# Low half of a third quarter of w_out on VectorE, and all operations in a new order

## The chip, the cores and the metric

The kernel runs on one core of a Trainium2 chip. The metric is the time on the device in microseconds (us), the median of several executions; lower is better. A core has five engines that work side by side and meet at semaphores: TensorE (PE, matrix products, with its weight loads shown apart as PEld), VectorE (DVE), ScalarE (ACT), GpSimd (POOL) and SyncE (SP), which here issues every DMA. Each engine runs its own instructions in the order in which they stand in the program.

## The reference

The inputs are q, k, v (8 batches, 8 heads, 576 positions, 64 wide), w_in (512 x 1024), w_out (1024 x 512) and g_ln (1024). k and v are averaged over groups of 8 positions, so that each head has 72 keys; then comes attention, and its output, 4608 rows of 512, goes through a SoLU layer:

```python
scores = scale * q @ k_pooled.T
attn = softmax(scores)
x = attn @ v_pooled                    # 4608 x 512 after the heads are put side by side
h = x @ w_in                           # 4608 x 1024
solu = h * softmax(h)
ln = (solu - mean(solu)) / sqrt(var(solu) + 1e-6) * g_ln
out = ln @ w_out                       # 4608 x 512
```

## The kernel before

The 4608 rows are worked on in 36 tiles of 128 rows. A group of nine tiles holds two batches: four tiles of the first, one mixed tile with the last 64 rows of both, four of the second. Every product that needs more than 16-bit accuracy is made of float16 halves: an operand X is kept as X_hi and X_lo = X - X_hi, and a product is the sum of hi·hi, lo·hi and hi·lo.

**A tile** goes through: `q_hi`, `q_lo`, `q_T` (split q, transpose it by DMA), `scores`, `s_max`, `s_sub`, `s_exp`, `e_sum`, `e_rec`, `e_mul` (softmax), `e_hi`, `e_lo`, `e_T` (split and transpose), `av` (attention times v), `x_hi`, `x_lo`, `mm1` in three parts of 16 matmuls (tile h in a buffer `hp`, of which there are two), `h_max`, `h_nb`, `h_exp`, `z_scale`, `z_mul`, `z_cen`, `z_hi`, `z_lo`, `z_T`, `z_var`, `n_u`, `n_f`, `mm2` in three parts, `o_evac`, `o_store`. Tiles overlap: scores of a tile run some tiles ahead of its `mm1`, and `mm2` some behind.

**The weights** arrive as 64-bit floats, seen as pairs of 32-bit words, a quarter (c = 0 to 3) at a time: `w_load` (1024 KB), then `w_exp`, `w_shift`, `w_tail`, `w_sgn`, `w_mul` make 32-bit floats of them; `w_bnd`, `w_rmax`, `w_par`, `w_all` and `wi_scale` or `wo_scale` find a power of two that bounds all four quarters. Then `w_hi` writes the high half. For the low half there are two ways:

- `w_res` and `w_lo`: TensorE forms w·scale - w_hi in PSUM, by a product with a diagonal matrix (`w_dg`, made by ScalarE) and one with minus the identity (`minus`), and ScalarE copies it to float16;
- `w_lod`: VectorE forms it directly, one `scalar_tensor_tensor` for each half of 512 columns, all three tensors in SBUF.

Which quarter takes which way is in the set `LO_DVE`: before, quarters 2 and 3 of w_out go by VectorE, all other six by TensorE. Pooled k and v of batch 0 are summed by TensorE (`pool_pe`, with copies `pool_ev` by ScalarE), those of later batches by GpSimd (`pool_kv`).

**The order** is written out by hand as a table: `ORDER[name]` gives each call of a step its place in one list of some 2080 steps. The steps are sorted by it and issued one after the other, so that the table alone sets what stands behind what on each engine. A step is one to some hundred instructions. SP's queue is in the same order, and a DMA that waits holds up all DMAs behind it. The tag "raw" has seven buffers, shared by four quarters of w_out, two of w_in and the raw k and v of each batch; a load into one waits until its last reader is done.

Of the kernel before, what the change touches and what calls it, by code (L numbers as in the profile page):

```python
# [30 lines left out]
        "a_unit.k": (39, 57, 211, 213, 451, 455, 657, 663, 882, 890, 1129, 1155, 1390, 1437, 1615,
        1616),
        "a_unit.v": (131, 134, 254, 261, 500, 503, 804, 805, 1027, 1029, 1180, 1181, 1481, 1482,
        1804, 1805),
        "av": (215, 257, 276, 333, 383, 463, 506, 573, 561, 661, 775, 702, 842, 893, 952, 977,
        1012, 1111, 1189, 1206, 1287, 1327, 1398, 1433, 1512, 1546, 1628, 1684, 1651, 1756, 1785,
        1852, 1920, 1939, 1997, 1972),
        "e_T": (221, 239, 275, 332, 402, 425, 572, 497, 628, 712, 641, 761, 825, 873, 933, 957,
        1078, 1145, 1146, 1248, 1263, 1356, 1406, 1476, 1495, 1557, 1647, 1634, 1718, 1748, 1851,
        1887, 1908, 1996, 1942),  # L40
# [18 lines left out]
        "e_sum": (91, 139, 185, 253, 311, 367, 412, 498, 437, 538, 655, 612, 704, 772, 817, 888,  # L59
        926, 1023, 1106, 1049, 1200, 1238, 1274, 1345, 1425, 1379, 1502, 1581, 1564, 1655, 1704,  # L60
        1784, 1824, 1864, 1954, 1917),
        "g_T": (93,),
        "g_all": (122,),
        "g_max": (96,),
        "g_par": (121,),
        "g_put": (94,),
        "h_bat": (245, 283, 679, 904, 1060, 1182, 1535, 1839),
        "h_exp": (265, 325, 362, 441, 457, 545, 614, 623, 697, 751, 857, 828, 936, 954, 1005,
        1037, 1151, 1185, 1258, 1300, 1384, 1402, 1486, 1510, 1612, 1618, 1679, 1796, 1720, 1832,
        1875, 1925, 1989, 1979, 2040, 2022),  # L70
        "h_max": (256, 305, 347, 411, 454, 525, 585, 619, 660, 719, 838, 777, 917, 941, 979, 1028,
        1130, 1159, 1231, 1268, 1309, 1389, 1456, 1489, 1551, 1610, 1673, 1733, 1703, 1798, 1846,
        1913, 1947, 1965, 2038, 2011),
# [161 lines left out]
def kernel(  # L235
# [48 lines left out]
    wo = const.tile([P, 2, CO, DM], F16, name="wo")  # L284
# [1073 lines left out]
    LO_DVE = {("wo", 2), ("wo", 3)}  # L1358
# [191 lines left out]
```

## Time and profile before

| | before |
|---|---|
| median of 3 executions | 487.48 us (487.16 to 487.89) |
| span of the profiled execution, first to last instruction | 483.6 us |
| what lies around the span, taken as median less span | 3.9 us |
| TensorE busy | 456.5 us |
| VectorE busy | 372.2 us |
| ScalarE busy | 335.2 us |
| GpSimd busy | 304.5 us |

The profile has no time of its own for the profiled execution beside its span. The three executions lie within 0.15% of each other, so the span and 3.9 us around it are read as one of them. A row of a timeline gives start, duration, engine, line, operation, written and read tiles, and in brackets the idle time before it with what ended it.

### The profile page before, as it was taken

Reading aid. Unit: us, or ns where it says so; the run is one execution under the profiler, and the core shown is the slowest. Engines: PE = TensorE matmul, PEld = TensorE weight load, DVE = VectorE, ACT = ScalarE, POOL = GpSimd, SP = SyncE. Lnnn points to the kernel's source line nnn. Section 1 sums busy time; section 2 is a strip of 40 time slices with the busy share of each in tenths; the row PEclk is TensorE's granted clock in tenths of the full one; section 3 lists DMA queues with packets and bytes.
Section 4 is the critical chain, followed back from the end, with each engine's and each line's share of the span. In section 5 each row is a group of like instructions: output and inputs, shape, how many; then the busy total and the mean of one; then the engine's idle time right before and its main releaser. Section 6 shows DMA issues by size and latency. Waiting matters only on the chain.

```text
span 483.6 us, 14740 instructions
## 1 busy us (share of the span) xinstructions
PE 456.5 (94%) x5976; PEld 287.7 (59%) x5976; DVE 372.2 (77%) x787; ACT 335.2 (69%) x557; POOL 304.5 (63%) x525
## 2 busy tenths in 40 slices
PE   1779899999999999999999999999999999999996
PEld 1655455655655556555556667666776666755553
DVE  5988999999889789878798867678878887462320
ACT  5598887677966688796677657587585697456361
POOL 3459737696697985858953597717758625643532
PEclk9989999999999999999999999999999999999999
DMA  8999389998999899999994999689899576861742
GB/s 309 395 354 225 86 114 219 196 193 138 213 237 213 209 173 207 204 229 229 161 215 111 215 245 172 126 136 243 167 229 190 115 137 117 138 142 24 153 108 69
DMA packets 197749, 88.92 MB, mean 184 GB/s; under 512 B 174121, under 2 KB 182321, under 8 KB 197169
## 3 DMA queue, kind: packets, MB, share of 16 engines
q1 hardware_dynamic: 197680, 87.98, 85.9%
q8 instruction: 47, 0.77, 0.6%
q14 instruction: 22, 0.17, 0.1%
HBM read 36.70 MB, written 9.44 MB: 95 GB/s over the span
## 4 chain that ended last, share of the span: by engine, by line
PE 78%; DVE 16%; DMA 2%; issue 2%; ACT 1%; SPq 0%; POOL 0%; ACTq 0%; DVEq 0%
PE op L274 35%; PE hp L274 31%; PE xp L999 4%; PE sc L274 3%; DMA kr<-in_k_dram 2%; DVE q L866 2%; DVE m L1041 1%; PE krps L410 1%; DVE sc L934 1%; DVE mx L920 1%; DVE sc L923 1%; DVE z L1073 1%; DVE e L949 1%; PE vrps L410 1%; PE res_wi L810 1%
## 5 line engine op out<-in xcount | busy, mean ns | idle before, releaser
L274 PE MATMUL hp<-wi,xT 128*64 128x512 f16 x1728 | 197.2, 379 | 2.8 <-DVE z L1073 1.4
L274 PE MATMUL op<-wo,zT 128*64 128x512 f16 x1728 | 197.2, 379 | 0.1
L274 PEld LDWEIGHTS <-xT 128*64 128x64 f16 x1728 | 106.6, 110 | 75.2 <-ACT xT L1008 2.0
L274 PEld LDWEIGHTS <-zT 128*64 128x64 f16 x1728 | 106.5, 110 | 70.6 <-DMA zT<-z 0.5
L1093 POOL TENSOR_TENSOR z<-z,z 128x512 f16<-128x512 f32 x71 | 82.0, 1167 | 67.9 <-ACT z L1087 66.4
L978 POOL TENSOR_TENSOR e<-e,e 128x512 f16<-128x512 f32 x36 | 42.2, 1173 | 39.7 <-ACT e L972 39.6
L1041 DVE TENSOR_REDUCE m<-hp 128x1 f32<-128x1024 f32 x36 | 43.8, 1217 | 23.1 <-PE hp L274 22.9
L1082 ACT ACTIVATE z<-z,sz 128x1024 f32<-128x1024 f32 x36 | 41.2, 1143 | 17.4 <-DVE z L1073 17.4
L1073 DVE SCALAR_TENSOR_TENSOR z<-hp,rs,z 128x1024 f32<-128x1024 f32 x36 | 46.1, 1280 | 9.1 <-ACT z L1052 7.9
L1052 ACT ACTIVATE z<-hp,nb,Hb 128x1024 f32<-128x1024 f32 x32 | 38.3, 1196 | 11.7 <-DVE nb L1044 9.1
L1151 ACT ACTIVATE osb<-op,f 128x512 f32<-128x512 f32 x36 | 24.5, 679 | 31.3 <-PE op L274 8.1
L1087 ACT ACTIVATE z<-z 128x1024 f16<-128x1024 f32 x36 | 37.7, 1050 | 0.9 <-DMA zT<-z 0.4
L1106 ACT ACTIVATE junk<-z 128x1024 f16<-128x1024 f32 x36 | 37.7, 1048 | 0.3
L400 POOL TENSOR_TENSOR vr<-vr 128x512 f32<-128x512 f32 (+3 forms) x42 | 36.9, 888 | 0.6
L400 POOL TENSOR_TENSOR kr<-kr 128x512 f32<-128x512 f32 (+3 forms) x42 | 36.7, 882 | 1.0 <-DMA kr<-in_k_dram 0.2
L920 DVE TENSOR_REDUCE mx<-sc 128x8 f32<-128x576 f32 x36 | 27.0, 750 | 12.9 <-PE sc L274 12.6
L934 DVE TENSOR_REDUCE sc<-sc 128x8 f32<-128x576 f32 x36 | 27.3, 759 | 12.2 <-ACT sc L930 12.1
L999 PEld LDWEIGHTS <-vb 128*64 128x64 f16 x960 | 28.9, 111 | 6.7 <-DVE vb L574 1.0
L1012 DVE SCALAR_TENSOR_TENSOR xT<-xp,xT 128x512 f16<-128x512 f32 x36 | 24.5, 681 | 8.9 <-ACT xT L1008 8.8
L999 PE MATMUL xp<-eT,vb 128*64 128x128 f16 (+1 forms) x960 | 31.0, 215 | 0.3 <-ACT e L975 0.3
L274 PEld LDWEIGHTS <-qT 128*64 128x64 f16 x1152 | 24.7, 114 | 9.9 <-ACT dg_wi L803 3.4
L1008 ACT ACTIVATE xT<-xp 128x512 f16<-128x512 f32 x36 | 21.2, 589 | 12.2 <-PE xp L999 12.2
(237 smaller groups left out, 621.3 us busy)
## 6 DMA issues: line engine op xcount, KB each, us to landing
kr<-in_k_dram SPq DMA_DIRECT2D x16, 512.0 KB
qr<-in_q_dram SPq DMA_DIRECT2D x16, 512.0 KB
vr<-in_v_dram SPq DMA_DIRECT2D x16, 512.0 KB
out_dram<-osb SPq DMA_DIRECT2D x32, 256.0 KB
wor<-in_moe_w_out_dram SPq DMA_DIRECT2D x4, 1024.0 KB
wo<-in_moe_w_in_dram SPq DMA_DIRECT2D x2, 1024.0 KB
wir<-in_moe_w_in_dram SPq DMA_DIRECT2D x2, 1024.0 KB
zT<-z SPq DMA_TRANSPOSE x72
```

The costliest lines, as they stand in the source:

```text
L274: nc.tensor.matmul(out[lo : lo + 64] if m > 64 else out, lhsT=lhsT[:, lo : lo + 64], **kw)
L400: nc.gpsimd.tensor_tensor(out=dst, in0=src[:, :, :n], in1=src[:, :, n : 2 * n], op=ALU.add)
L934: nc.vector.tensor_reduce(out=tl[i]["r0"], in_=s_view(i), axis=AX.X, op=ALU.add)
L978: nc.gpsimd.tensor_tensor(out=e_main(i, 1), in0=e_src(i)[0], in1=e_main(i, 0), op=ALU.subtract)
L999: nc.tensor.matmul(xp[64 * e : 64 * e + 64, c, lo:hi], lhsT=vb[b % 2][:, n, c, e], rhs=eT[:, 2 * c + e if n < 2 else H + e, lo:hi], start= ...
L1041: nc.vector.tensor_reduce(out=small(i, "m"), in_=tl[i]["hp"], axis=AX.XY, op=ALU.max)
L1052: nc.scalar.activation(z, t["hp"], AF.Exp, bias=t["nb"], scale=hsc(i, 0), accum_out=small(i, "se"))
L1073: nc.vector.scalar_tensor_tensor(out=t["z"], in0=t["hp"], scalar=t["rs"], in1=t["z"], op0=ALU.mult, op1=ALU.mult, accum_out=small(i, "sz"),)
L1082: nc.scalar.activation(t["zf"], t["zf"], AF.Identity, bias=t["sz"], scale=-float(DFF))
L1087: nc.scalar.activation(t["z16"][:, 0], t["zf"], AF.Copy)
L1093: eng.tensor_tensor(out=t["z16"][:, 1, fs], in0=t["zf"][:, fs], in1=t["z16"][:, 0, fs], op=ALU.subtract)
L1106: nc.scalar.activation(junk, t["zf"], AF.Square, scale=DFF**-0.5, accum_out=small(i, "V"))
```

## The change

`LO_DVE` also holds quarter 1 of w_out. For that quarter the program no longer has `w_dg` (two ScalarE instructions), `w_res` (TensorE) and `w_lo` (one ScalarE instruction), and has two `w_lod` on VectorE. The table `ORDER` is another one: from the first step to about the middle of the list steps stand in other places; the last 141 of TensorE's 338 steps, the last 246 of VectorE's 716 and the last 160 of ScalarE's 439 follow each other as before. Line numbers of the new program are 5 higher from the end of the table on. Of the table two lines are shown:

```diff
-        "w_lod.wo": (344, 324, 321, 316),
-        "w_res.wo": (210, 173),
+    "w_lod.wo": (217, 215, 258, 319, 303, 318),
+    "w_res.wo": (197,),
...
     POOL_SIGN = {(nm, c) for nm in ("wi", "wo") for c in range(4)}
-    LO_DVE = {("wo", 2), ("wo", 3)}
+    LO_DVE = {("wo", 1), ("wo", 2), ("wo", 3)}
     Q_ABS = {("b", b) for b in range(0)}
```

SP at the start of the program, before (`wo` is the buffer that two quarters of w_in are loaded into, `wir` are the other two, `wor` quarters of w_out, `kr`, `vr`, `qr` raw k, v and q of batch 0):

```order
L623 DMA wo<-in_moe_w_in_dram 128x2048 x2
L360 DMA kr_158<-in_k_dram 64x512
L623 DMA wir_169<-in_moe_w_in_dram 128x2048
L356 DMA kr_158<-in_k_dram 128x2x512 x2
L376 DMA qr_182<-in_q_dram 128x4x256 x2
L623 DMA wir_222<-in_moe_w_in_dram 128x2048
L623 DMA wor_288<-in_moe_w_out_dram 128x2x1024
```

The same place now:

```order
L628 DMA wo<-in_moe_w_in_dram 128x2048 x2
L365 DMA kr_146<-in_k_dram 64x512
L628 DMA wir_160<-in_moe_w_in_dram 128x2048
L381 DMA qr_162<-in_q_dram 128x4x256
L361 DMA kr_146<-in_k_dram 128x2x512
L738 DMA kp_88<-in_moe_g_ln_dram 8x128
L381 DMA qr_162<-in_q_dram 128x4x256
L628 DMA wir_167<-in_moe_w_in_dram 128x2048
L361 DMA kr_146<-in_k_dram 128x2x512
L628 DMA wor_269<-in_moe_w_out_dram 128x2x1024
```

The last part of k of batch 0 has moved behind both halves of q and the last quarter of w_in.

VectorE from the scale of q of batch 0 (`sq`) to the low half of its transposed keys (`kT`, line 536 before), before (`amx_k` is the largest pooled k, `u_wi`, `u_wo`, `wir`, `wor` are weights on the way to 32-bit floats):

```order
L472 RECIPROCAL sq('b', 0)_206<-pq('b', 0)_205 128x1
L430 TENSOR_REDUCE amx_k<-kp_87 128x1
...
L657 SCALAR_TENSOR_TENSOR wir_222<-wir_222,u_wi_224 128x1024
L686 TENSOR_REDUCE g_wi<-bnd_wi 128x1
L638 TENSOR_SCALAR u_wo_290<-u_wo_290 128x1024
...
L657 SCALAR_TENSOR_TENSOR wor_288<-wor_288,u_wo_290 128x1024
L690 TENSOR_REDUCE gm_wi<-g_wi 128x1
...
L536 SCALAR_TENSOR_TENSOR kT_300<-kTp_230,sk_216,kT_300 128x576
L920 TENSOR_REDUCE mx_373<-sc_320 128x8
```

The same place now:

```order
L477 RECIPROCAL sq('b', 0)_221<-pq('b', 0)_220 128x1
L871 SCALAR_TENSOR_TENSOR q_0_229<-qr_162,sq('b', 0)_221,q_0_229 128x8x64
...
L871 SCALAR_TENSOR_TENSOR q_3_251<-qr_162,sq('b', 0)_221,q_3_251 128x8x64
L745 COPY g_sb<-gT 128x8
L691 TENSOR_REDUCE g_wi<-bnd_wi 128x1
...
L435 TENSOR_REDUCE amx_k<-kp_87 128x1
...
L662 SCALAR_TENSOR_TENSOR wor_269<-wor_269,u_wo_271 128x1024
L643 TENSOR_SCALAR u_wo_295<-u_wo_295 128x1024
L541 SCALAR_TENSOR_TENSOR kT_325<-kTp_314,sk_307,kT_325 128x576
```

The largest pooled k now stands behind the third split of q and the bound of w_in, and the keys' low half behind one more shift of a quarter of w_out.

TensorE from the last residual of w_in to the first `av`, before (`eTp` is the transposed softmax of tile 0, `res_wo` the residuals, `xp` the output of `av`):

```order
L813 MATMUL res_wi_629<-wi,minus 128x512
L810 MATMUL res_wo_635<-wor_369,dg_wo_556 128x512
...
L883 MATMUL eTp_648<-ident_101,e_0_93 128x128
...
L274 MATMUL gk_661<-identb,amx_k 64x128
...
L810 MATMUL res_wo_718<-wor_288,dg_wo_641 128x512
...
L999 MATMUL xp_727<-eT_659,vb_91 64x128
```

The same place now:

```order
L818 MATMUL res_wi_625<-wi,minus 128x512
...
L888 MATMUL eTp_634<-ident_101,e_0_93 128x128
...
L279 MATMUL sc_651<-kT_325,qT_647 64x72
...
L279 MATMUL gk_688<-identb,amx_k 64x128
...
L815 MATMUL res_wo_697<-wor_269,dg_wo_550 128x512
...
L1004 MATMUL xp_707<-eT_645,vb_91 64x128
```

Behind the last residual of w_in one of the two residual blocks of w_out is gone, and scores of tile 2 (`sc_651`), which stood ahead of that residual, now stand behind the transposition. On VectorE the new pair of `w_lod` stands between `e_mul` of tile 2 and `q_lo` of tile 4; those of quarters 2 and 3 follow later.

## Rows read from the trace of the kernel before

**Rows 1.** Stretches of the span: busy time of each engine, granted clock, DMA.

```profile
core 0: us, PE busy (x) PEld busy (x) DVE busy (x) ACT busy (x) POOL busy (x), PEclk, DMA share, GB/s
0.00:28.00 28.00, 11.08 (x126) 10.18 (x128) 21.21 (x46) 17.03 (x22) 10.67 (x18) 0.99 0.95 358
28.00:58.00 30.00, 27.12 (x304) 16.26 (x299) 26.53 (x56) 26.71 (x45) 22.45 (x25) 0.96 0.83 211
58.00:88.00 30.00, 27.71 (x376) 16.67 (x378) 29.57 (x61) 22.59 (x39) 16.03 (x23) 1.00 0.90 171
88.00:118.00 30.00, 29.07 (x450) 17.50 (x448) 28.80 (x64) 22.15 (x40) 24.26 (x45) 1.00 0.90 170
118.00:240.00 122.00, 121.95 (x1666) 72.11 (x1664) 103.61 (x217) 92.23 (x156) 95.26 (x163) 1.00 1.05 205
240.00:360.00 120.00, 120.00 (x1668) 81.73 (x1666) 96.86 (x211) 82.88 (x146) 77.67 (x138) 1.00 0.91 186
360.00:460.00 100.00, 100.00 (x1228) 63.14 (x1225) 62.70 (x130) 62.77 (x104) 51.41 (x99) 1.00 0.69 129
460.00:484.00 24.00, 19.62 (x182) 10.09 (x178) 2.87 (x8) 8.86 (x13) 6.71 (x18) 1.00 0.34 89
```

**Rows 2.** A short stretch at the first scores.

```profile
27.60:29.00 1.40, 1.33 (x40) 1.29 (x41) 0.12 (x1) 1.40 (x2) 1.40 (x2) 0.50 1.06 399
```

**Rows 3.** Timeline of TensorE: start us, us, instructions, idle time before and its end.

```profile
13.10 5.64 PE L410 MATMUL krps<-kr,ident 128*128 128x128 f32 x32 [1.56 <-DMA kr<-in_k_dram]
...
27.67 1.17 PE L274 MATMUL sc<-kT,qT 128*64 128x72 f16 x32 [3.19 <-DVE kT L536]
...
32.46 5.11 PE L410 MATMUL vrps<-vr,ident 128*128 128x128 f32 x48
37.50 0.71 PE L274 MATMUL sc<-kT,qT 128*64 128x72 f16 x32
...
48.79 1.06 PE L810 MATMUL res_wo<-wor,dg_wo 128*128 128x512 f32 x2
...
50.80 0.38 PE L813 MATMUL res_wo<-wo,minus 128*128 128x512 f16 x1
52.08 0.72 PE L883 MATMUL eTp<-ident,e 128*128 128x128 f16 x10 [0.90 <-ACT wi L824]
...
58.15 1.92 PE L274 MATMUL hp<-wi,xT 128*64 128x512 f16 x16 [0.17 <-ACT xT L1008]
```

**Rows 4.** Timeline of ScalarE: first weight quarter, a residual's copy, a pair of diagonals.

```profile
5.78 1.12 ACT L634 ACTIVATE u_wi<-wo 128x1024 f32<-128x1024 f32 x1 [3.71 <-DMA wo<-in_moe_w_in_dram]
...
51.91 1.02 ACT L824 ACTIVATE wo<-res_wo 128x1024 f16<-128x1024 f32 x1
52.82 0.70 ACT L803 ACTIVATE dg_wo<-ident,sg_wo 128x128 f32<-128x128 f32 x2
```

**Rows 5.** Timeline of VectorE, from q of batch 0 to the keys.

```profile
17.45 1.22 DVE L442 TENSOR_REDUCE amx_q<-qr 128x1 f32<-128x1024 f32 x1 [0.27 <-DMA qr<-in_q_dram]
...
19.36 0.49 DVE L430 TENSOR_REDUCE amx_k<-kp 128x1 bf16<-128x320 f32 x1
...
20.40 0.74 DVE L866 SCALAR_TENSOR_TENSOR q<-qr,sq('b', 0)_206,q 128x512 f16<-128x512 f32 x1
...
23.95 0.69 DVE L638 TENSOR_SCALAR u_wo<-u_wo 128x1024 int32<-128x1024 int32 x1
...
24.68 1.23 DVE L657 SCALAR_TENSOR_TENSOR wor<-wor,u_wo 128x1024 int32<-128x1024 int32 x1
...
26.71 0.81 DVE L536 SCALAR_TENSOR_TENSOR kT<-kTp,sk,kT 128x576 f16<-128x576 f32 x1
```

**Rows 6.** Timeline of VectorE: low halves of w_out formed by it.

```profile
77.71 0.73 DVE L818 SCALAR_TENSOR_TENSOR wo<-wor,sg_wo,wo 128x512 f16<-128x512 f32 x1
...
78.68 1.55 DVE L818 SCALAR_TENSOR_TENSOR wo<-wor,sg_wo,wo 128x512 f16<-128x512 f32 x1
```

**Rows 7.** Timeline of GpSimd at the same time.

```profile
78.52 1.16 POOL L978 TENSOR_TENSOR e<-e,e 128x512 f16<-128x512 f32 x1 [2.90 <-ACT e L972]
```

More of the change, by code (lines that the diff above doesn't have):

```diff
@@ L32 @@
[L32 to L39, printed above, removed]
@@ L64 @@
[L64 to L72, printed above, removed]
@@ new lines @@
+    "h_max": (241, 271, 324, 392, 425, 478, 525, 604, 631, 710, 828, 776, 886, 950, 988,
+        1042, 1119, 1143, 1222, 1268, 1309, 1386, 1455, 1488, 1550, 1609, 1672, 1732, 1702,
+        1797, 1844, 1912, 1946, 1964, 2037, 2010),
+    "h_mix": (362, 918, 1242, 1855),
+    "h_nb": (251, 281, 336, 399, 429, 487, 527, 606, 640, 712, 836, 778, 902, 963, 998,
+        1054, 1151, 1144, 1237, 1270, 1330, 1390, 1482, 1489, 1572, 1616, 1673, 1757, 1707,
+        1821, 1847, 1913, 1947, 1965, 2038, 2011),
@@ new lines @@
+    "s_scale": (89, 285, 366, 528, 705, 781, 1037, 1178, 1216, 1541, 1695, 1754),
+    "s_sub": (96, 155, 196, 228, 287, 365, 391, 493, 428, 572, 697, 615, 643, 756, 801, 867,
+        904, 958, 1113, 1039, 1185, 1221, 1277, 1340, 1421, 1371, 1452, 1576, 1544, 1622,
+        1696, 1753, 1818, 1861, 1948, 1899),
+    "scores": (85, 153, 189, 225, 274, 349, 383, 484, 426, 559, 694, 613, 637, 749, 789,
+        863, 895, 954, 1105, 1036, 1170, 1207, 1264, 1327, 1407, 1369, 1450, 1574, 1542,
+        1619, 1681, 1731, 1815, 1858, 1940, 1897),
@@ new lines @@
+    "v_hi": (140, 165, 322, 345, 575, 577, 823, 833, 1061, 1063, 1249, 1227, 1506, 1521,
+        1807, 1808),
+    "v_lo": (178, 180, 340, 377, 621, 591, 843, 838, 1091, 1076, 1250, 1302, 1507, 1577,
+        1817, 1822),
+    "v_rep": (149, 353, 582, 862, 1165, 1298, 1497, 1845),
+    "v_x": (177, 179, 344, 356, 590, 578, 845, 844, 1123, 1081, 1300, 1231, 1624, 1539,
+        1827, 1820),
+    "w_all.wi": (61,),
+    "w_all.wo": (143,),
+    "w_bnd.wi": (5, 21, 24, 56),
+    "w_bnd.wo": (105, 106, 107, 130),
@@ new lines @@
+    "w_dg.wi": (66,),
+    "w_dg.wo": (151,),
+    "w_exp.wi": (3, 16, 22, 36),
+    "w_exp.wo": (55, 64, 88, 95),
+    "w_hi.wi": (137, 86, 78, 92),
+    "w_hi.wo": (175, 214, 239, 302),
+    "w_lo.wi": (166, 150, 136, 182),
+    "w_lo.wo": (229,),
+    "w_load": (0, 1, 6, 11, 54, 63, 82, 83),
+    "w_lod.wo": (217, 215, 258, 319, 303, 318),
+    "w_mul.wi": (14, 31, 32, 44),
+    "w_mul.wo": (76, 98, 213, 295),
+    "w_par.wi": (60,),
+    "w_par.wo": (142,),
+    "w_pwi": (244,),
+    "w_pwo": (338,),
@@ new lines @@
+    "w_res.wi": (164, 148, 87, 181),
+    "w_res.wo": (197,),
+    "w_rmax.wi": (57,),
+    "w_rmax.wo": (131,),
+    "w_sgn.wi": (13, 30, 26, 43),
+    "w_sgn.wo": (62, 97, 141, 221),
+    "w_shift.wi": (4, 17, 23, 38),
+    "w_shift.wo": (70, 73, 93, 99),
+    "w_tail.wi": (12, 18, 25, 42),
+    "w_tail.wo": (72, 91, 94, 134),
+    "wi_scale": (65,),
+    "wo_scale": (144,),
+    "x_hi": (203, 231, 265, 304, 386, 452, 481, 554, 536, 662, 780, 699, 824, 881, 914, 990,
+        1022, 1087, 1174, 1230, 1273, 1332, 1398, 1433, 1512, 1546, 1628, 1701, 1657, 1756,
+        1787, 1852, 1920, 1949, 1998, 1975),
```

252 lines of the change are left out of this document (108 added, 144 removed), and 90 rows, old and new, of the table ORDER.

## The prediction

> **What bounds the kernel now.** I read the table of busy times by stretch first, because the average share of an engine mixes stages with different limits [rows 1]. From 118 to 460 us TensorE is busy in all but 0.05 of 342 us: there only the sum of TensorE's work counts, and nothing that another engine does shortens it. The last stretch holds 24 us with 19.62 us of TensorE, and ends with the last tile's copy and store; its steps follow each other as before. TensorE's idle time is ahead of that: 28.00 - 11.08 = 16.9 us up to 28 us, 2.9 us from 28 to 58, 2.3 us from 58 to 88 and 0.9 us from 88 to 118. So two things can move the end: less work for TensorE, and less idle time of it before 118 us.
>
> Next I read who ended the idle time [rows 3]. Pooled keys start late, since they wait for a transfer; the first scores wait 3.19 us for VectorE, which writes the keys' low half; the transposition of tile 0's softmax waits 0.90 us for ScalarE. VectorE is busy 29.57 of the 30 us from 58 to 88, and 28.80 of the next 30 [rows 1]: in the two stretches where TensorE still has gaps, VectorE has none to give, and the change gives it more work.
>
> **The change part by part.** The sum is made on the profiled execution, 483.6 us of span and 3.9 us around it, 487.5 us, which is the median of the runs shown.
>
> *TensorE's residual goes.* The block for quarter 1 of w_out runs from 48.79 us to 50.80 + 0.38 = 51.18 us [rows 3], 2.39 us; neighbouring blocks overlap a little, so I take 2.3 us. From 118 us on nothing can absorb this but a new wait: -2.3 us. The bounds are -2.4 us and, if each microsecond comes back as a wait, 0.
>
> *ScalarE* loses one copy of 1.02 us and a pair of diagonals of 0.70 us [rows 4], 1.7 us. It was busy 26.71 of 30 us from 28 to 58 [rows 1], so this lets its later copies start earlier. I count it at nothing by itself; its worth is in the waits below.
>
> *VectorE* gains two instructions. The same instruction took 0.73 us at 77.71 and 1.55 us at 78.68 us [rows 6]. The long one ran beside a GpSimd subtraction of 1.16 us that began at 78.52 us, and before that one GpSimd had stood idle for 2.90 us [rows 7]. So the pair costs 1.5 us with GpSimd idle and 3.1 us beside it. I take 1.5 to 2, as the new place, between softmax of tile 2 and the split of q of tile 4, has GpSimd waiting for the same tile's copies for a good part.
>
> The Trainium skill says why, and against this change: in "SBUF — State Buffer", section "Who interferes with whom", a VectorE instruction whose two inputs are both in SBUF competes with a GpSimd instruction that reads SBUF, and whichever comes second waits for the first. The two rows agree in kind, 1.55 us beside GpSimd against 0.73 us. The copy that goes read PSUM on another engine, so by the rule the exchange makes a pair that could not be blocked into a pair that can; taken as always blocked it is the second rival below, taken as never blocked the sum stays as it is.
>
> *The loads move.* Before, the first quarter of w_in, 1024 KB, was there at 5.78 us [rows 4], and the second half of q, with 5248 KB issued up to and with it (three quarters, k, q), at 17.45 us [rows 5]: 11.67 us for 4224 KB, 2.83 us for each 1024 KB. Now the last part of k stands behind all of q and the last quarter of w_in, 6272 KB with itself, so I expect it at 17.45 + 2.83 = 20.3 us. TensorE then sums it in half of 5.64 us [rows 3], to 23.1 us, where it was done at 13.10 + 5.64 = 18.7 us: 4.4 us later. On VectorE, before, the largest k began 0.6 us behind that, at 19.36 us, and the keys' low half ended at 26.71 + 0.81 = 27.5 us [rows 5], 8.2 us in all. Of what lay between, two splits of q (0.74 each), a last step of a weight quarter (1.23), a shift (0.69) and the bound's reduction now stand ahead, and one shift (0.69) comes in: 8.2 - 0.7 x 2 - 1.2 - 0.4 = about 5 us. The first scores should start at 23.1 + 0.6 + 5.1 = 28.8 us at the earliest; with the hops to ScalarE I take 29.5 us against 27.67 us. In exchange TensorE does ahead of them what it did behind: two fifths of v's pooling (5.11 us [rows 3] for three parts of sizes 2, 2 and 1, so 2.0 us) and two small products, together 2.5 us. Net -0.7 us, with bounds of -2.5 us (scores as early as before) and +3 us (k lands later, third rival).
>
> *The clock.* At 27.60 to 29.00 us the granted clock is 0.50 [rows 2], the lower of its two levels (1.2 instead of 2.4 GHz), after a stretch in which TensorE had little to do. The first scores take 1.17 us there and 0.71 us ten microseconds later [rows 3], and the mean clock of 0.96 from 28 to 58 us is 1.2 us of full speed lost [rows 1]. With v's part put into that gap the fall may not come, or come elsewhere. I take half, -0.6 us; bounds -1.2 and +0.6 us.
>
> *Waits from 28 to 118 us.* Up to the first `mm1` I put the steps in their new order one behind another, each with its row's duration. TensorE finds three waits: the largest v (its last part is behind 5248 KB more than k, 14.5 us at 2.83 us for 1024 KB, so lands near 35 us and is then pooled, copied, reduced), the bound of w_out right behind it, and x of tile 0, whose copy on ScalarE stands behind tile 2's exponential and so behind VectorE's s_sub of tile 2. Together some 4 us against the 2.9 us before [rows 1]: +1.0 us, between 0 and +2.5. From 58 to 118 us the new order brings the steps that `mm1` needs (`x_lo`, `h_max`, `z_mul` of tiles 0 to 3) ahead of the preparation of batch 1's v and the splits of later q, so that of 3.2 us of idle time some can go; the pair of 1.5 to 3.1 us stands against it. I take -0.4 us, between -2.9 and +2.5.
>
> Sum: -2.3 - 0.7 - 0.6 + 1.0 - 0.4 = -3.0 us: span 480.6 us, time 484.5 us.
>
> **The rivals.** *All gaps close.* The new order was laid so that VectorE never keeps `mm1` waiting, and the clock stays up: -2.3 - 0.7 - 1.2 + 1.0 - 2.9 = -6.1 us, 481.4 us. For it: ScalarE has 1.7 us less, and the largest waits before were single ones. Against it: hops between engines are not in such a count, and VectorE has no slack from 58 to 88 us.
>
> *VectorE takes what TensorE gives.* Both new instructions run beside GpSimd, 3.1 us, and TensorE waits for them in 58 to 118 us: -2.3 - 0.7 + 1.0 + 2.5 = +0.5, 488.0 us with the clock as before, 487.4 us with half of it. For it: VectorE is full there. Against it: the steps moved behind `mm1` are worth more than the pair.
>
> *The keys come late.* The transfer of the last part of k shares the engines with what is queued behind it (two quarters of w_out) and lands at 26 us instead of 20.3. Then each step from the largest k on is 5.7 us later, and TensorE, which runs in order, waits: -3.0 + 5.7 = +2.7, 490.2 us. It turns to slower from a landing 3 us late, at 23.3 us. For it: the transfers are at a share of 0.95 all the time up to 28 us [rows 1]. Against it: before, transfers were used in the order in which they were issued.
>
> **How the numbers follow.** Chances: the forecast, 483 to 486.5 us, 0.58; all gaps close 0.13; VectorE takes it 0.15; late keys 0.14. I put the time at 484.5 us. The range reaches from 481.9 to 488.4 us, which holds the forecast, most of the second rival and the slower half of the first; the likeliest case alone is 483 to 486.5 us. Taken as no change is what lies within 0.2%, about 1 us, which is what a measurement of this kernel can tell: up to 486.5 us is faster, from 488.5 us slower. Faster is the forecast and the first rival, 0.71; the same is the second rival but for a tail, 0.14; slower the third and that tail, 0.15.
>
> **What would show it.** After 118 us the timeline of TensorE must again be without gaps, and its total 2.3 us smaller: else the first term is wrong. The first scores should start near 29.5 us, and v's middle part be pooled ahead of them; a start beyond 32 us is the late keys. The granted clock just there tells the third term. The first `mm1`, at 58.15 us before [rows 3] with scores of tile 3 done, should start near 56 us without them. Two low halves of quarter 1 at 0.7 us each near 58 us, with no wait of TensorE for VectorE over 1 us behind them, speak for the forecast, 1.5 us each and such a wait for the second rival. A result above 487 us would mean that idle time before 118 us grew by more than 2 us.

## The result and the profile after

The changed kernel takes 493.77 us (median of 4 executions, 490.94 to 494.46) against 487.38 us; the ratio is 1.0123, 95% interval [1.0092, 1.0153]. It is slower, and the forecast of 484.5 us was wrong in sign. Run once more for the last experiments it took 490.73 us (6 executions, 489.49 to 492.55), ratio 1.0089 [1.0065, 1.0112]. Its first four executions lie 3.5 us apart and those of the kernel before 0.7, though 17 later ones of the kernel before lie 3.4 us apart too (485.35 to 488.70). The two profiles of the changed kernel, of spans 492.6 and 489.1 us, differ in their front. I call them the first and the second profile; the instructions are the same. One execution reported below, of the eighteenth kernel, fell into a slower state of the chip and is left out of its median.

The kernel before needs one correction. I had read its span of 483.6 us as the median with 3.9 us around it. Later executions that have both a time and a span lie 1.7 to 1.8 us apart, one of them 485.35 us with a span of 483.6. So the profile of before shows an execution of about 485.4 us (an estimate from these), 2 us faster than the median, and differences of spans to it, 9.0 and 5.5 us here, are larger than those of the medians, 6.4 and 4.4 us.

Busy times by stretch, first profile, same columns as [rows 1]:

```profile
0.00:28.00 28.00, 13.66 (x106) 12.57 (x108) 19.57 (x45) 15.66 (x20) 11.14 (x18) 1.00 0.95 358
28.00:58.00 30.00, 24.95 (x237) 15.65 (x235) 26.27 (x45) 20.82 (x32) 13.64 (x13) 0.89 0.73 192
58.00:88.00 30.00, 27.58 (x383) 16.36 (x377) 29.46 (x61) 24.83 (x41) 18.93 (x22) 1.00 0.59 114
88.00:118.00 30.00, 29.01 (x447) 18.75 (x445) 28.70 (x60) 23.24 (x41) 25.35 (x49) 1.00 1.02 199
118.00:240.00 122.00, 117.68 (x1619) 75.49 (x1615) 101.02 (x222) 88.41 (x154) 91.66 (x157) 1.00 1.03 201
240.00:360.00 120.00, 120.00 (x1664) 82.02 (x1661) 98.03 (x212) 82.41 (x143) 83.42 (x143) 1.00 0.92 184
360.00:460.00 100.00, 100.00 (x1290) 64.80 (x1288) 65.39 (x136) 66.82 (x112) 54.30 (x99) 1.00 0.70 133
460.00:493.00 33.00, 28.61 (x266) 14.80 (x262) 6.55 (x15) 12.36 (x17) 10.14 (x27) 0.97 0.48 116
```

The second profile, the stretches that differ:

```profile
0.00:28.00 28.00, 13.69 (x123) 12.38 (x124) 20.58 (x47) 16.38 (x20) 11.26 (x18) 1.00 0.96 359
28.00:58.00 30.00, 24.02 (x268) 14.32 (x268) 28.65 (x53) 24.56 (x39) 16.73 (x17) 0.94 0.73 199
58.00:88.00 30.00, 28.37 (x410) 17.16 (x408) 29.49 (x61) 23.47 (x40) 19.19 (x28) 1.00 0.72 141
...
118.00:240.00 122.00, 116.74 (x1600) 76.11 (x1598) 99.58 (x220) 88.08 (x151) 90.87 (x156) 1.00 1.04 200
240.00:360.00 120.00, 119.52 (x1658) 82.44 (x1656) 99.31 (x208) 82.12 (x144) 82.58 (x141) 1.00 0.89 184
```

Stretch length less TensorE's busy time gives its idle time; the busy time of the whole span is the sum over all stretches:

| TensorE, us | before | first profile | second profile |
|---|---|---|---|
| idle, 0 to 28 | 16.9 | 14.3 | 14.3 |
| idle, 28 to 58 | 2.9 | 5.1 | 6.0 |
| idle, 58 to 118 | 3.2 | 3.4 | 2.6 |
| idle, 118 to 360 | 0.05 | 4.3 | 5.7 |
| busy, whole span | 456.55 | 461.50 | 456.59 |
| span | 483.6 | 492.6 | 489.1 |

The work should have fallen by 2.3 us to 454.3. It stands 7.2 and 2.3 us above that, and no instruction was added to TensorE: the same matmuls took longer. TensorE's timeline in the front, first profile (compare [rows 3]):

```profile
14.59 3.78 PE L415 MATMUL krps<-kr,ident 128*128 128x128 f32 x16 [3.16 <-DMA kr<-in_k_dram]
...
21.46 3.73 PE L415 MATMUL krps<-kr,ident 128*128 128x128 f32 x16
...
33.68 0.71 PE L279 MATMUL sc<-kT,qT 128*64 128x72 f16 x32
...
43.37 0.25 PE L279 MATMUL gv<-identb,amx_v 128*64 128x128 bf16 x2 [2.92 <-DVE amx_v L435]
...
45.54 2.08 PE L815 MATMUL res_wi<-wo,dg_wi 128*128 128x512 f32 x2
...
62.71 1.49 PE L279 MATMUL hp<-wi,xT 128*64 128x512 f16 x12 [0.75 <-ACT xT L1013]
```

The same places in the second profile:

```profile
21.45 3.00 PE L415 MATMUL krps<-kr,ident 128*128 128x128 f32 x16
...
30.12 0.71 PE L279 MATMUL sc<-kT,qT 128*64 128x72 f16 x32 [0.41 <-DVE kT L541]
...
38.06 0.25 PE L279 MATMUL gv<-identb,amx_v 128*64 128x128 bf16 x2 [1.16 <-DVE amx_v L435]
...
57.57 3.64 PE L279 MATMUL hp<-wi,xT 128*64 128x512 f16 x32 [0.75 <-ACT xT L1013]
```

Up to 21.45 us the two agree within 0.2 us; the first part of k takes 3.78 us in both. Then the last part of k takes 3.73 us in one and 3.00 in the other: TensorE's clock comes up within that part in the second profile, and only near 33.7 us in the first. By the first `mm1` that is 62.71 against 57.57 us, where the kernel before has 58.15 [rows 3]. So there is a slow front and a quick one, 5.1 us apart. In the quick one the changed kernel reaches the first `mm1` 0.6 us sooner, but with the 0.7 us of scores of tile 3 still to do, which stood ahead of it before: it is level, where the forecast had `mm1` start near 56 us. From 118 us on it then loses 5.7 us, 5.0 of them in three waits:

```profile
146.41 0.71 PE L279 MATMUL sc<-kT,qT 128*64 128x72 f16 x32 [1.52 <-DVE pq('m', 1)_2475 L466]
...
174.22 0.86 PE L1004 MATMUL xp<-eT,vb 128*64 128x128 f16 x24 [1.97 <-DMA eT<-e]
...
210.50 1.70 PE L279 MATMUL hp<-wi,xT 128*64 128x512 f16 x14 [1.55 <-DVE z L1078]
```

The first profile has the same three, 1.57, 0.97 and 1.58 us, near 150, 177 and 213 us.

### The profile page after: what moved, and what is told of

Same layout as the page of the kernel before. It is cut to its first block, busy times and chain, and to the rows that moved or that the text cites. A ratio compares the mean times of both kernels' runs of the same rounds, so it can differ in the third digit from the quotient of the medians.

```text
span 492.6 us, 14701 instructions
## 1 busy us (share of the span) xinstructions
PE 461.5 (94%) x5970; PEld 300.4 (61%) x5970; DVE 375.0 (76%) x789; ACT 334.6 (68%) x554; POOL 308.6 (63%) x525
## 4 chain that ended last, share of the span: by engine, by line
PE 64%; DVE 21%; ACT 4%; DMA 4%; issue 3%; POOL 2%; SPq 1%; ACTq 0%; DVEq 0%
PE op L279 29%; PE hp L279 25%; PE xp L1004 3%; PE sc L279 2%; DVE q L871 2%; DVE z L1078 2%; DVE sc L939 2%; DVE e L954 2%; DVE amx_q L447 1%; DVE m L1046 1%; DVE mx L925 1%; DMA qm<-in_q_dram 1%; DVE sc L928 1%; DMA eT<-e 1%; DMA wo<-in_moe_w_in_dram 1%
## 5 line engine op out<-in xcount | busy, mean ns | idle before, releaser
L279 PEld LDWEIGHTS <-xT 128*64 128x64 f16 x1728 | 110.5, 110 | 71.8 <-ACT xT L1013 2.6
L279 PEld LDWEIGHTS <-zT 128*64 128x64 f16 x1728 | 110.7, 110 | 67.5 <-DMA zT<-z 0.2
L983 POOL TENSOR_TENSOR e<-e,e 128x512 f16<-128x512 f32 x36 | 43.7, 1213 | 40.2 <-ACT e L977 35.7
L977 ACT ACTIVATE e<-e 128x512 f16<-128x512 f32 x36 | 22.3, 620 | 13.6 <-DVE e L954 11.9
```

The lines of the kernel that those rows point to most:

```text
L279: nc.tensor.matmul(out[lo : lo + 64] if m > 64 else out, lhsT=lhsT[:, lo : lo + 64], **kw)
L983: nc.gpsimd.tensor_tensor(out=e_main(i, 1), in0=e_src(i)[0], in1=e_main(i, 0), op=ALU.subtract)
```

## The experiments

Medians are of the runs named; a ratio is to executions of the kernel before taken beside them (their medians were 486.3 to 487.0 us).

**1. The pair alone, in the old order.**

```diff
-    LO_DVE = {("wo", 2), ("wo", 3)}
+    LO_DVE = {("wo", 1), ("wo", 2), ("wo", 3)}   # ORDER of before; the two w_lod behind e_mul of tile 3
```

> The kernel before with one part of the change alone: the third quarter of w_out gets its low half from two VectorE instructions (set behind e_mul of tile 3), and the residual's matmuls, the scaled identities and ScalarE's copy are gone; every other operation keeps its old place. Theory A (the new order of the front and of the stretch 118 to 240 us costs the 6.4 us, the VectorE pair is harmless): TensorE loses 2.3 us of work, so 485 us, ratio 0.995, at worst 488. Theory B (the pair itself costs: VectorE is late and TensorE waits for it): 490 us or more. By A the first mm1 starts near 56 us, by B a gap of TensorE stands behind the pair near 66 us or at the first mm2.

Measured: 490.96 us, ratio 1.0082 [1.0064, 1.0100]. So theory A, by which only the new order costs, fell. TensorE's timeline:

```profile
51.09 0.25 PE L279 MATMUL gk<-identb,amx_k 128*64 128x128 bf16 x2 [1.19 <-DVE amx_k L435]
53.79 0.44 PE L279 MATMUL vr<-vr,sel 128*64 128x64 f16 x16 [2.46 <-DVE pk L497]
...
55.77 1.92 PE L815 MATMUL res_wo<-wor,dg_wo 128*128 128x512 f32 x2
...
59.73 3.64 PE L279 MATMUL hp<-wi,xT 128*64 128x512 f16 x32 [0.17 <-ACT xT L1013]
...
78.20 0.44 PE L279 MATMUL vr<-vr,sel 128*64 128x64 f16 x16 [1.64 <-DVE xT L1017]
```

VectorE's instruction that ends the longer wait, here and then in the kernel before:

```profile
53.45 0.29 DVE L497 TENSOR_REDUCE pk<-gk 128x1 f32<-128x128 f32 x1
```

```profile
53.10 0.29 DVE L492 TENSOR_REDUCE pk<-gk 128x1 f32<-128x128 f32 x1
```

VectorE comes to it 0.35 us later than before, not sooner (that execution was 0.39 us late already at the scores of tile 2): it sets the pace here, and the residual had lain beside it. Where 2.3 us of work stood, TensorE now waits 1.19 + 2.46 us instead of 0.90 + 0.47, 2.3 us more, and behind the hole the last residual takes up to 1.92 us a pair instead of 1.06: the removed work comes back as a wait and a slow stretch.

**2. The new order with the residual put back.**

```diff
-    LO_DVE = {("wo", 1), ("wo", 2), ("wo", 3)}
+    LO_DVE = {("wo", 2), ("wo", 3)}   # ORDER of after; w_dg, w_res, w_lo of quarter 1 beside those of w_in's last quarter, its w_hi and the other w_lod a few steps off
```

> The changed kernel with the residual path put back for the third quarter (scaled identities, four matmuls, ScalarE's copy, each set beside those of the last quarter of w_in), all else in the new order. Theory A (order costs): 493.8 + 2.3 = 496 us, ratio 1.018. Theory B (the pair costs): back to about 487.5 us, ratio 1.00.

Measured: 494.13 us, ratio 1.0168 [1.0104, 1.0231]. The order costs by itself, as A said. The three waits behind 118 us are there without the pair on VectorE, 3.60 us and then 0.89 and 1.58 us near 177 and 213 us, so the pair is not their cause:

```profile
151.19 0.71 PE L279 MATMUL sc<-kT,qT 128*64 128x72 f16 x32 [3.60 <-DVE pq('m', 1)_2482 L466]
```

Against the changed kernel's ratios of 1.0123 and 1.0089 the pair in the residual's place gives 2.2 to 3.8 us within the new order, but the intervals overlap, so neither the size nor, strictly, the sign is settled.

**3 and 4. Half of one order, half of the other.** Ahead of the first `mm1` the steps stand as in one kernel, behind it as in the other; the pair is in both.

```diff
 e3:  steps ahead of mm1(0) as in before, all others as in after
 e4:  steps ahead of mm1(0) as in after, all others as in before
```

> VectorE pair kept; operations that stood ahead of the first mm1 in the old order stand there in the old order, all that follow stand in the new one. Theory A splits the loss in two: 4.6 us by the first mm1 (62.71 instead of 58.15 us), 4.3 us in three gaps between 118 and 240 us. Then this kernel keeps the second part alone: first mm1 near 56 us, gaps near 150, 178 and 213 us (shifted 6 to 7 us earlier), about 489.5 us, ratio 1.004. A rival (C: the three gaps are only a late effect of the slow front, since their loads are issued by work that came late) gives 485 us and no such gaps.

> VectorE pair kept; operations that stand ahead of the first mm1 in the new order stand there in the new order, all that follow stand in the old one. Theory A: the front's loss alone: slower TensorE up to 33.7 us, the wait of 2.9 us near 41 us and the slow stretch behind it, first mm1 near 62.7 us, no gaps from 118 to 240 us, about 489.5 us, ratio 1.004 to 1.008. Rival C (the gaps come from the slow front): about 493 us with gaps there.

Measured: 490.54 us, ratio 1.0093 [1.0058, 1.0127], and 497.33 us, 1.0217 [1.0175, 1.0259]. In the third kernel the three waits are there although its front is the old one, so they are not a late effect of a slow front:

```profile
144.56 0.71 PE L279 MATMUL sc<-kT,qT 128*64 128x72 f16 x32 [1.58 <-DVE pq('m', 1)_2475 L466]
...
171.98 0.86 PE L1004 MATMUL xp<-eT,vb 128*64 128x128 f16 x24 [1.29 <-DMA eT<-e]
...
208.27 1.92 PE L279 MATMUL hp<-wi,xT 128*64 128x512 f16 x16 [1.59 <-DVE z L1078]
```

The fourth's time says nothing on the front: its seam itself makes waits of up to 2.5 us between 57 and 78 us. But its profile, with the new front and the old steps behind it, has no wait of 0.3 us or more from 118 us on, as A expected.

**5, 6 and 7. What of the loss in the old order is the hole, what the pair.**

```diff
 e5:  as e1, and w_dg, w_res of quarter 1 kept (result unused), w_lo gone
 e6:  as e1, but w_lo of quarter 1 copies the 32-bit weights, and no w_lod for it
 e7:  as e1, and on VectorE and ScalarE:
-     q_scale 3, v_lo(0,0), e_sum 2, v_lo(0,1), e_rec 4, a_all k 1
+     q_scale 3, v_lo(0,0), a_all k 1, e_sum 2, v_lo(0,1), e_rec 4
-     s_exp 2, w_lo wi 3, w_dg wo 0
+     w_dg wo 0, s_exp 2, w_lo wi 3
```

> The old order with the VectorE pair, as in the first experiment, but the residual's four matmuls and the scaled identities of the third quarter are kept, and nothing reads their result; of the old path only ScalarE's copy is gone. Theory W (between 44 and 58 us VectorE and ScalarE set the pace, the residual lay beside them, and taking it out opens a hole in which TensorE loses its clock): TensorE is busy again from 48.8 to 51.2 us, the last quarter's residual takes 1.06 us a pair and not 1.92, the first mm1 starts at 58.2 to 58.5 us and not at 59.74, and the time is 1.5 us under the 490.96 of the pair alone: 489.5 us; what is left over 487 is the pair on VectorE. Rival T (TensorE's work counts on the path): 2.3 us of work more, first mm1 at 62 us, 493 us.

> The old order without the residual of the third quarter and without the VectorE pair: ScalarE's copy stands at its old place but reads the 32-bit weights, so that the third quarter's low half is not computed. Theory W: the hole alone is left, first mm1 near 59.7 us, and the delay stays near 1.6 us where with the pair it grew to 2.8 us at tile 3: 488.5 to 489 us, ratio 1.003 to 1.005. Rival P (the pair on VectorE is all of the loss): 485 us, ratio 0.995.

> The old order with the VectorE pair; VectorE reduces the gathered maximum of batch 1's k (0.29 us) two instructions sooner and ScalarE writes the last quarter's scaled identities ahead of the exponent of tile 2. Theory W: the hole of 2.46 us ahead of the gather of v shrinks to about 0.8 us, the last residual runs at 1.06 us, and the first mm1 starts near 58.2 us, since its tile comes from e of tile 0 by way of VectorE and ScalarE, not earlier: 1.5 us under the pair alone, 489.5 us. Rival T: TensorE's shorter queue shows once the hole is closed, first mm1 near 56 us, 487 us.

Measured: 489.43 us, ratio 1.0043 [1.0024, 1.0061]; 489.03 us, 1.0028 [1.0004, 1.0052]; 489.55 us, 1.0055 [1.0036, 1.0073]. All three times are within 0.1 us of what theory W gave. TensorE in the sixth, which has neither residual nor pair for this quarter:

```profile
52.70 0.25 PE L279 MATMUL gk<-identb,amx_k 128*64 128x128 bf16 x2 [1.34 <-DVE amx_k L435]
55.26 0.64 PE L279 MATMUL vr<-vr,sel 128*64 128x64 f16 x16 [2.31 <-DVE pk L497]
55.83 2.08 PE L815 MATMUL res_wo<-wor,dg_wo 128*128 128x512 f32 x2
...
62.11 3.64 PE L279 MATMUL hp<-wi,xT 128*64 128x512 f16 x32 [0.17 <-ACT xT L1014]
```

It leaves out the third quarter's low half, does less and is still slower than before (of the 4.0 us that its first `mm1` is late, 1.9 stood already at the scores of tile 2, near 47 us): in the old order taking the residual away costs 1.4 us by the ratio (0.2 to 2.5 by its interval) where it should give 2.3, and the pair on top of it, e1 less e6, 1.9 us by the medians and 2.6 by the ratios. In the fifth, with the residual's matmuls kept, the last residual takes 1.17 and 1.06 us a pair. W missed one mark there: the first `mm1` starts at 60.50, not 58.2 to 58.5 us, because ahead of 47 us that execution had already lost 1.7 us (the first residual at 1.91 us a pair, a difference between executions that the seventh kernel shows too). In the seventh the hole shrank to 0.71 us as expected, but the residual still ran slow (1.89 us a pair), so that mark was missed as well; and the wait of 1.64 us near 78 us stayed. So the times bear out that the hole takes back what the residual gives; that the clock falls because of the hole's length is not shown.

**8, 9 and 10. Keep TensorE busy in the front.** Matmuls of the identity by itself, results unused, set into TensorE's waits:

```diff
+    for _ in range(n):
+        nc.tensor.matmul(dst, lhsT=ident, rhs=ident, start=True, stop=True)
 e8:  in after, ahead of pool_pe k 2, k 1, q_Tp, a_par v, w_par wo:        n = 3, 7, 3, 8, 3
 e9:  in before, ahead of pool_pe k 2, k 1, a_par k, w_par wi, scores 0:   n = 14, 3, 3, 4, 8
 e10: those of e9 in e7
```

> The changed kernel with 24 matmuls of the identity by itself (128x128, 32 bit) set into five waits of TensorE between 8 and 45 us (3, 7, 3, 8 and 3 of them), their results unused. Theory C (the front is slow because the split pooling of k and the wait of 2.9 us let TensorE's clock fall): the first and the middle part of k's pooling at 275 ns a matmul instead of 421, the transposes of k 1.3 us instead of 2.37, first scores near 31.8 us instead of 33.68, the second quarter of w_in's residual near 1.06 us a pair instead of 2.08, first mm1 near 60 us instead of 62.71, time about 491 us. Rival D (VectorE and the loads pace the front, the slow matmuls are only how TensorE fills it): first mm1 within 0.5 us of 62.71, time 493 to 494.5 us.

> The kernel before with 32 matmuls of the identity by itself (14, 3, 3, 4 and 8 of them) in five waits of TensorE ahead of the first scores, their results unused. Theory C (the clock in the front is a cost of its own): k's pooling wholly at 275 ns a matmul, the first scores 0.7 us long instead of 1.17 and the first residual 1.06 us a pair instead of 1.88, so 2 us off TensorE ahead of 33 us, of which VectorE, busy 13.5 of 14 us from 44 to 58 us, lets 0.5 to 1.5 us through: 485.5 to 486.5 us. Rival D: the front is paced by loads and VectorE, no change, 487 us.

> The old order with the VectorE pair and the two moves of the seventh experiment (sooner scale of batch 1's k, sooner scaled identities), and the same 32 matmuls of the identity in the front as in the ninth. If the pair cost only through the clock and the hole it left, this is the first version with less work on TensorE and no slow stretch: 485 to 486 us. If VectorE's 1.5 us of added work stay on the path near tile 3 (a gap of 1.6 us near 77 us is still there), 487.5 to 488.5 us.

Measured: 495.00 us, ratio 1.0170 [1.0117, 1.0223]; 489.38 us, 1.0037 [1.0014, 1.0060]; 489.42 us, 1.0050 [1.0032, 1.0068]. In the eighth the front is quick:

```profile
21.20 2.00 PE L415 MATMUL krps<-kr,ident 128*128 128x128 f32 x16
...
57.69 3.64 PE L279 MATMUL hp<-wi,xT 128*64 128x512 f16 x32 [0.75 <-ACT xT L1013]
```

The part of k that took 3.73 us takes 2.00, and the first `mm1` is 5.0 us earlier: the slow front is TensorE's clock. That the idle matmuls brought the clock up is shown for the first part of k alone, 3.08 us here and 3.78 in all seven profiles of this front without them. The last part can be as quick without any, as in the thirteenth kernel below, which has the changed kernel's steps up to there and its first `mm1` at 57.00 us:

```profile
21.07 2.00 PE L415 MATMUL krps<-kr,ident 128*128 128x128 f32 x16
```

The time did not fall. Between 94 and 152 us the lead goes, and the largest piece of it goes in one VectorE instruction beside a run of GpSimd's; VectorE first, then GpSimd at the same time:

```profile
112.08 5.40 DVE L871 SCALAR_TENSOR_TENSOR q<-qr,sq('b', 2)_1735,q 128x512 f16<-128x512 f32 x1
```

```profile
112.17 1.16 POOL L1098 TENSOR_TENSOR z<-z,z 128x512 f16<-128x512 f32 x1
113.29 1.16 POOL L983 TENSOR_TENSOR e<-e,e 128x512 f16<-128x512 f32 x1
114.40 0.30 POOL L986 TENSOR_TENSOR e<-e,e 128x64 f16<-128x64 f32 x1
114.67 2.27 POOL L1098 TENSOR_TENSOR z<-z,z 128x512 f16<-128x512 f32 x2
```

That split of q takes 0.74 us elsewhere [rows 5]. In the second profile, whose front is as quick, the same split begins beside the same GpSimd steps and is held far less, and the lead stays up to the wait near 146 us:

```profile
112.33 1.37 DVE L871 SCALAR_TENSOR_TENSOR q<-qr,sq('b', 2)_1706,q 128x512 f16<-128x512 f32 x1
```

The ninth and tenth, too, were slower than before: the ninth's first scores start at 28.80 instead of 27.67 us, behind its own idle matmuls, and its first `mm1` 0.7 us late. Its first scores took 0.71 us and its first residual 1.15 us a pair, as theory C said, but k's pooling 6.53 us and not less than the 5.64 before: that mark was missed. Theory C holds in part for the front and fell as a way to gain time.

**11, 12, 13 and 16. The three waits behind 118 us.**

```diff
 SyncE:   + load_qm 1 ahead of k_T 2 (was behind it, three loads of k, a z_T, two q_T and a store)
 SyncE:   + e_T of tile 10 ahead of z_T(8, 1)                    # e11 and e12 only
 GpSimd:  + pool_kv(4, v, 1, 0) and (4, v, 1, 1) behind z_lo(10, 0) (were ahead of e_lo 15)
 e12, e16: and the idle matmuls of e8
```

> The changed kernel with three things moved: the load of the third mixed q (SyncE) is issued ahead of the transpose of batch 2's k, the transposing DMA of e of tile 10 ahead of one of z, and GpSimd's first two additions over a part of batch 4's v stand behind the low half of z of tile 10. Theory M (the three gaps near 150, 177 and 213 us are these three queues' order): the gaps go, 4.1 us less, 489.7 us. Rival N (the gaps stand there because VectorE or the DMA engines are full, and come back a little later): over 492 us.

> The changed kernel with the three moves of the eleventh experiment and the identity matmuls of the eighth. With those matmuls alone the first mm1 came 5.0 us earlier, and all of it was lost by 158 us (a VectorE instruction of 5.4 us beside GpSimd at 112 us, then waits at 119, 133 and 149 us). If each loss has its own cause: 489.7 less 2 to 5 us, 485 to 488 us. If the stretch from 100 to 160 us is paced by VectorE, GpSimd and the loads in any case, the front's gain is lost again: 489.5 to 490.5 us.

> The changed kernel with two of the three moves: the load of the third mixed q earlier on SyncE, and GpSimd's two additions over batch 4's v behind the low half of z of tile 10. In the eleventh kernel the lag to the changed kernel fell by 3.2 us more than its front gave, before the third move's gap of 7.6 us. Theory M (queue order makes these gaps): 493.8 less 3.1, 490.7 us; 487 us if most runs have the quick front (first scores near 30.3 us and not 33.7). Rival N (the loss comes back elsewhere): 493 to 494 us.

> The changed kernel with the two moves and the 24 matmuls of the identity in its front. Theory C and M together: every run has the quick front (first mm1 at 57.7 to 60.4 us instead of 62.7) and the two gaps are gone: 486.5 to 488.5 us. If the stretch from 100 to 160 us sets its own pace: 490 to 491 us.

Measured: 497.72 us, ratio 1.0224 [1.0197, 1.0252]; 499.81 us, 1.0283 [1.0231, 1.0335]; 489.26 us, 1.0046 [1.0021, 1.0071]; 491.86 us, 1.0086 [1.0047, 1.0125]. In the eleventh the second move was ill set. It puts the transposing DMA of e of tile 10 not only ahead of one of z but also ahead of GpSimd's step that writes the low half of that e. So the DMA carries an old low half, GpSimd waits for it to land before it can write, and through GpSimd's `n_f` and ScalarE's copy `mm2` waits too:

```profile
172.82 1.15 POOL L983 TENSOR_TENSOR e<-e,e 128x512 f16<-128x512 f32 x1 [8.88 <-DMA eT<-e]
```

```profile
178.08 3.29 PE L279 MATMUL op<-wo,zT 128*64 128x512 f16 x16 [7.64 <-ACT osb L1156]
```

Without that move the thirteenth is 4.5 us under the changed kernel's first median. The twelfth has the same move and the same wait, 5.24 us, so neither says what an earlier transpose of e is worth. The sixteenth shows again that the idle matmuls do not help: it is slower than the thirteenth, which has none, and its first `mm1` comes at 58.96 us, not sooner than 57.00.

**14. The pair on GpSimd.**

```diff
 as e7, and for quarter 1:
-        nc.vector.scalar_tensor_tensor(...)
+        nc.gpsimd.tensor_scalar(out=w, in0=w, scalar1=scale, scalar2=None, op0=ALU.mult)
+        nc.gpsimd.tensor_tensor(out=lo, in0=w, in1=hi, op=ALU.subtract)
```

> As the seventh kernel (old order, hole half closed), but the third quarter's low half is made by GpSimd in four instructions (scale in place, subtract) at the same place, so VectorE has neither the pair nor anything else more than before. Theory W2 (with the hole closed, what the pair costs is VectorE's 1.5 us near tile 3): the gap of 1.64 us near 77 us is gone and the time is 1.5 us or so under the seventh kernel's 489.55: 487.5 to 488 us. Rival S (GpSimd's four instructions of about 1.2 us stall VectorE's instructions with two inputs in SBUF by as much): 489.5 us or more.

Measured: 489.17 us, ratio 1.0048 [1.0020, 1.0077], as the seventh within its interval. The time lies between the two forecasts; by the trace it is rival S: the wait near 78 us is still 1.48 us, with no pair on VectorE. GpSimd's four instructions took 1.67, 1.58, 1.73 and 1.16 us, and VectorE's next two with inputs in SBUF 1.66 and 1.37 us where 0.75 and 0.47 are usual.

**15. A known shift.**

```diff
 before, and ahead of mm1(0):
+    3 matmuls of the identity by itself, 0.83 us
```

> The kernel before with three matmuls of the identity by itself (0.83 us) directly ahead of the first mm1, at full clock, results unused; nothing else is changed. Theory F (the old order has no gap after 118 us because it fits its own timing; a shift of TensorE against the other engines makes new waits): the lag grows from 0.7 us at the first tile to 1.5 to 4 us at the end, 488.5 to 490.5 us. Rival A (work added on TensorE costs its length): 487.7 us, lag 0.7 to 0.9 us from the first tile to the last.

Measured: 487.78 us, ratio 1.0017 [1.0002, 1.0033]. Rival A: added work on TensorE cost its own length, 0.83 us by the ratio (0.1 to 1.6 by its interval). Theory F, that the old order breaks under any shift, fell; the profiled execution did gain one wait of 0.93 us, near 354 us, but the median does not bear it out.

**17 and 18. The changed kernel and the two moves, side by side.**

```diff
 e17: after, unchanged        e18: e13, unchanged
```

> The changed kernel once more, unchanged. If its front is the same in every execution, the first mm1 stands near 62.7 us again and the median at 493 to 494.5 us. If the front has a quick and a slow version (clock up at about 28 us, or only at 33.7 us), its runs lie apart by up to 4 us, and this profile may show a first mm1 near 57 to 59 us with the gaps near 150, 178 and 213 us still there, shifted by as much.

> The changed kernel with the two moves, once more, beside the changed kernel itself. If the moves are worth the two gaps they close: 2.5 to 3.2 us under the other kernel of this call. If they only moved the gaps (in the profile the lag grew by 1.2 us at 158 us and 1.0 us at 214 us, and 1.0 us came back by 232 us): 1 to 1.5 us under it.

Measured: 490.73 us, ratio 1.0089 [1.0065, 1.0112], and 488.44 us (11 executions), 1.0058 [1.0033, 1.0083]. The seventeenth gave the second profile above, with the quick front and all three waits. The longest waits of the eighteenth between 118 and 240 us:

```profile
171.96 0.86 PE L1004 MATMUL xp<-eT,vb 128*64 128x128 f16 x24 [0.99 <-DMA eT<-e]
...
207.25 1.92 PE L279 MATMUL hp<-wi,xT 128*64 128x512 f16 x16 [0.59 <-DVE z L1078]
...
225.04 0.71 PE L279 MATMUL sc<-kT,qT 128*64 128x72 f16 x32 [0.67 <-DMA kT<-kr]
```

The wait for the mixed q is gone, the other two are smaller, and one of 0.67 us is new: 3.0 us less span in the profiles, of which the waits are 2.5, and 2.3 us less in the medians, 1.5 by the ratios, whose intervals overlap a little. So the moves are worth some 1.5 to 3 us, and the rest of the 4.5 us of the thirteenth lies, as far as profiles show, in the front, which happened to be slow in the changed kernel's first one. What makes the wait for the transposed e near 174 us is left open.

No kernel here beats the one before.

## Why the prediction was wrong

Three terms failed: the residual taken at its length, the clock taken as a gain, and nothing put behind 118 us. In their place the runs showed a hole that gave nothing back in the old order (it cost 1.4 us), slow matmuls of 2.3 to 7.2 us in the front, and new waits of 4.3 to 5.7 us. Step by step, with the terms as they were put.

*The residual, -2.3 us, "From 118 us on nothing can absorb this but a new wait".* It took the worth of the work from 118 us on, where TensorE has no wait, but the residual stands at 48.79 us, in a stretch where VectorE is busy 26.53 and ScalarE 26.71 of 30 us [rows 1]. Experiments 1, 5 and 6 show the residual lying beside that chain: taken out of the old order it gives nothing back and leaves a hole, so it came out at the far bound that I had given it, 0, and worse. In the new order the medians have the right sign (experiment 2), but its size is not settled.

*ScalarE at nothing, the pair at 1.5 to 2 us.* The pair took 0.75 us an instruction at 64.73 us in the first profile and 0.74 in the second, as forecast. In the old order it cost 1.9 us or more (e1 less e6); its mark is TensorE's wait of 1.64 us near 78 us, which the kernels with the pair in the old order have and those without it, before and e6, do not.

*The loads, first scores at 29.5 us.* The last part of k was in time: TensorE starts on it at 21.45 us without a wait, so the late keys, my third rival, are excluded. (By its own numbers that rival gives 487.5 us for a landing 3 us late; slower, 488.5 us, would be 4 us late.) In the quick front the scores start at 30.12 us, 0.6 us late. In the slow one they start at 33.68, and the reason is the next step.

*The clock, -0.6 us with +0.6 as the worst.* This was the first step that failed. Before, k's pooling ran as one piece and the clock rose within it: 32 matmuls in 5.64 us [rows 3]. Cut in two, with waits of 3.16 and 1.20 us around the parts, the first half takes 3.78 us in every profile without idle matmuls, and the second from 2.00 us (13, 18) over 3.00 (second profile) to 3.73 (first profile, 2, 4). I had looked for the clock only where the granted clock showed 0.50 [rows 2] and did not ask what my own timeline of the new loads did to the stretch before it. With the matmuls behind it (the keys' transposition, v's part, the residual at 2.08 us) the slow front costs 7.2 us of TensorE's time and the quick one 2.3 us. Experiment 8 shows that filled waits quicken the first half of k (3.08 us); since the second half is sometimes quick without that, what keeps the clock down there is not shown.

*Waits from 28 to 58 us, +1.0 us.* They came to +2.2 and +3.1 us, within and beyond the upper end of +2.5. VectorE's last step on a weight quarter was held twice beside GpSimd in the slow front. At 36.96 us it took 3.04 us, and VectorE came to the largest v 2.4 us behind v's pooling instead of 0.6 in the quick front: that is in TensorE's wait of 2.92 us. At 45.03 us it took longer still, though TensorE, whose residual ran slow meanwhile, waited only 0.34 us behind it:

```profile
45.03 4.13 DVE L662 SCALAR_TENSOR_TENSOR wor<-wor,u_wo 128x1024 int32<-128x1024 int32 x1
```

```profile
42.51 5.51 POOL L405 TENSOR_TENSOR kr<-kr 128x512 f32<-128x512 f32 x6 [3.60 <-DMA kr<-in_k_dram]
```

It takes 1.23 us otherwise [rows 5]. I had applied the rule of the Trainium skill ("SBUF — State Buffer", section "Who interferes with whom") to the pair alone, where both profiles of the changed kernel show no stall (the second of the two took 1.64 us in e11 and e18), and not to the instructions that the order had newly put beside GpSimd.

*58 to 118 us, -0.4 us.* +0.2 and -0.6 us: right.

*Nothing behind 118 us.* This is the step that cost most in the quick front: 4.3 and 5.7 us (0.5 of it behind 240 us) where I put 0. The rows show 122 us without a wait before [rows 1], and I took that as a property of the stretch ("only the sum of TensorE's work counts"). It was a property of the order: the new one is another order up to the middle of the list. It puts two of GpSimd's additions over v ahead of a low half of z that they stood behind, and lets VectorE take the maximum of the mixed q 7 us sooner, where its load, issued behind two transposes of q and three loads of k, has not landed. VectorE in the second profile, then before:

```profile
140.49 0.69 DVE L447 TENSOR_REDUCE amx_m<-qm 128x1 f32<-128x512 f32 x1 [2.25 <-DMA qm<-in_q_dram]
```

```profile
147.67 0.67 DVE L442 TENSOR_REDUCE amx_m<-qm 128x1 f32<-128x512 f32 x1
```

Experiments 2 and 3 show that the three waits come with the order of the steps behind the first `mm1`, with either front and without the pair; 4 agrees, though its TensorE is so late that this alone could hide them; and 13 and 18 show that two moves take part of them away, some 2.5 us in the profiles.

The sum for the quick front, in span: clock and residual together 0.0 instead of -2.9, idle time ahead of 118 us -0.2 instead of -0.1, behind it +5.7 instead of 0: +5.5 us. The slow front adds 4.9 us of slow matmuls and saves 1.4 us of waits: +9.0 us. Both are against the one profiled execution of the kernel before, about 2 us under its median. What decides between the fronts, with the same instructions up to 21.45 us, is not known.

## What to carry to other kernels

Work taken from the engine with the highest busy share is worth its length only where no other engine sets the pace; look at the waits a microsecond after the place, and ask what the engine does in the hole. A stretch without waits is a property of the order that was measured: when the order is new, go through each queue's loads and each shared buffer in that stretch again, and put a range of several microseconds on it. Where a long run of matmuls is split in two with waits around the parts, look at the durations of equal matmuls in both parts and behind them: here they stayed at the slow level in some executions until 33.7 us, and one profile did not tell.

## What the runs showed of the hardware

- A VectorE instruction with two inputs in SBUF can be held for a whole run of GpSimd instructions, not for one alone: 5.40 us instead of 0.74 beside five of them that ended at 116.94 us, 4.13 instead of 1.23 us beside six additions that ended at 48.02. It need not be: beside the same runs of the second profile the same two took 1.37 and 1.93 us. What decides is not shown.
- The granted clock reads 0.99 and 1.00 for the first 28 us of the two kernels, although 16 equal matmuls there take 3.78 us in one place and 2.00 us in another (thirteenth kernel); it is the durations that tell the level.
- The same program has fronts that lie 5.1 us apart at the first `mm1`.
